# Retention and a PReLU feed-forward layer on one core: a weight piece loaded by columns, a pass-on begun on two banks, two of seven products exchanged

## The chip, the core and the metric

The kernel runs on one core of a Trainium2 chip. A core has a matrix engine (TensorE, PE in the profile, its weight loads PEld), a vector engine (VectorE, DVE), a scalar engine (ScalarE, ACT), a general engine (GpSimd, POOL), and SyncE (SP), which here only issues transfers. The metric is the device time of one execution in microseconds (us), as the median of several runs; lower is better.

## The reference

```python
# q, k, v: (4, 8, 768, 64);  w_in: (512, 2048);  w_out: (2048, 512);  alpha: (2048,)
gamma = 1.0 - 2.0 ** (-5.0 - np.arange(H))
for t in range(S):
    state = gamma * state + einsum('bhd,bhe->bhde', k[:, :, t], v[:, :, t])
    y[:, :, t] = scale * einsum('bhd,bhde->bhe', q[:, :, t], state)
x = y.transpose(0, 2, 1, 3).reshape(3072, 512)
h = x @ w_in
g = np.maximum(h, 0.0) + alpha * np.minimum(h, 0.0)
out = g @ w_out
```

A linear attention with a decaying state gives a row of 512 values for each of 3072 tokens; two matrix products with a PReLU between them follow.

## The kernel before

**Blocks and stages.** The 3072 tokens are six blocks of 512 (`NBLK`, L40). Attention is done in chunks of 128 tokens, written in pairs; the first four pairs (`w`, functions that begin with `u`) are handled as units of 256 tokens. Its result y lands in two banks of the accumulator memory PSUM, and is passed on to `xT[n]`, the block's input of the first layer, as f16. The first layer of block n (`ffn1`, `ffn1_half`, `ffn1_mix`) multiplies `w_in_all` by `xT[n]` in tiles of 128 hidden units, and the PReLU is a ScalarE instruction (`hm`) with a VectorE one (`gt`). The second layer multiplies `gt` by `w_out_all`.

**PSUM.** There are eight banks. Four rotate under the tags p0 to p3: `ps(tag="pb")` (L96) takes the next one and counts in `turns`, and `bank(i, name)` (L93) names one by its number, modulo four. The other four rotate under the tag pa for attention.

**Loads.** All inputs go through a ring of twelve staging buffers (`ring`, L102) by transfers that SP issues in program order. `load_first` (L1076) brings the first 512 columns of w_in as two transfers of 256 columns, each with all four groups of 128 rows. `load_w("wi", 1)` (L1052) brings the next 512 columns, the second piece, as two transfers of two row groups with all 512 columns. `cast_first` and `cast_w` (L1082, L1065) turn the staged f32 into f16, one instruction a row group, on the engines in the list given. The second piece's casts are three on POOL (L1172) and one on ScalarE, which stands before the last part of block 0's first tiles (L1183). `ffn1(0, lo=4)` (L1197) then goes through tiles 4 to 15: tiles 4 to 7 use the second piece, 8 to 11 the third.

**The pass-on.** `out_second` (L317) and `uout_copy` (L573) write y's two banks, ya (X = 0) and yb (X = 1), to `xT`. Where part of the state's contribution was computed ahead in a third and fourth bank and copied out (`z_copy`, L601), each bank is passed on in two halves: VectorE adds z to one (`put_y`, L611; L584) and ScalarE copies the other (L612; L585), first for X = 0, then for X = 1. Where there is no z, ScalarE copies both whole (L608; L591). The tile framework orders two engines that read the same bank.

**Seven products.** For blocks 1 to 5 the second layer is done by `seven(n)` (L802): a 2 by 2 scheme over halves of tokens, hidden units and output columns that needs seven products in place of eight, with sums of `gt` (`g_sums`, L782: which = 0 is sm[0], 1 is sm[1] made from it, 2 is `third`, 3 changes part of `gt` in place) and sums of w_out (`wsum`). A `product` is 16 matmuls of 128 by 128 by 256. Before:

```python
b, a = bank(k, "ops"), bank(k + 1, "ops")
yield from product(b, A(0, 0), W(0, 0), True)     # P1
s1 = kept(b, "um0")
yield from product(a, A(0, 1), W(1, 0), True)     # P2
store = put(0, 0, a, s1)
yield from product(b, sm[1], wsum[1])             # P3
u2 = kept(b, "um0")
```

`kept` (L825, instruction L827) is ScalarE's copy of a bank to SBUF; `put` (L833) is VectorE's sum into an output buffer (L839), and returns the store (L843), on SP or, in the last block, partly on ScalarE. P4 (sm[0]·wsum[0]) goes into c, bank k+1; P5 (third·wsum[2]) adds to b; P6 goes into d, bank k+2; P7 adds to c.

**Order.** Everything is ordered by hand. `seven(n)` is a generator that yields after each matmul, and `tick(gen, m)` (L1027) advances it by m matmuls; between the ticks stands the attention work for the next block. What follows a product (a copy, a sum, a store) is issued when the generator is next advanced. In block 1 the ticks are 17, 16, 31, then the outputs of the first pair (`out_first`, `out_second`) with states and scores of the second pair, then 6, 23, the second pair's outputs, 7 and the rest. In blocks 2 to 4 they are 34, 26, the first pair's outputs, 6, 15, 17, the second pair's outputs, 7 and the rest (L1346 to L1415). In block 5 there is no attention, and the products follow each other after 34 ticks and four VectorE sums. Each engine runs its instructions in program order.

Of the kernel before, what the change touches and what calls it, by code (L numbers as in the profile page):

```python
# [11 lines left out]
COPY = mybir.ActivationFunctionType.Copy  # L12
RELU = mybir.ActivationFunctionType.Relu
MULT = mybir.AluOpType.mult
ADD = mybir.AluOpType.add
# [4 lines left out]
def kernel(  # L20
# [10 lines left out]
    nc = tc.nc  # L31
# [10 lines left out]
    scale = 1.0 / np.sqrt(D)  # L42
# [50 lines left out]
    def bank(i, name, dt=FP, n=512):  # L93
        return psp.tile([128, n], dt, tag=f"p{i % 4}", bufs=1, name=name)
# [222 lines left out]
    def out_second(us):  # L317
        if us[0] not in zs:
            out_states(us, 1)
        z = zs.pop(us[0], None)  # L320
        yv, _ = ys.pop(us[0])
        nb, at = divmod(us[0], UB)
        if at == 0:
            xT[nb] = sbp.tile([128, 2, NP, TB // 2], F16, tag="xT", bufs=2, name=f"xT{nb}")
        to = xT[nb][:, at // 2].rearrange("p a (t x j) -> p a t x j", x=2, j=64)
        for X in range(2):
            put_y(to[:, :, :, X, :], yv[X], X, z and z[X])

    ustaged, ukq, ukT, uv, um = {}, {}, {}, {}, {}

# [242 lines left out]
    def uout_copy(w, shared=False, z=None):  # L573
        y = uy.pop(w)[0]
        nb, at = divmod(2 * w, UB)
        if at == 0:
            xT[nb] = sbp.tile([128, 2, NP, TB // 2], F16, tag="xT", bufs=2, name=f"xT{nb}")
        for X in range(2):
            lo = C * X
            to = xT[nb][:, at // 2, :, lo : lo + C].rearrange("p a (n j) -> p a j n", j=2)  # L580
            src = y[X].rearrange("p (a j n) -> p a j n", j=2, n=64)
            if z and z[X]:
                own, other = slice(2 * X, 2 * X + 2), slice(2 - 2 * X, 4 - 2 * X)
                nc.vector.tensor_tensor(out=to[:, other], in0=src[:, other], in1=z[X], op=ADD)  # L584
                nc.scalar.activation(  # L585
                    out=to[:, own], in_=src[:, own], func=COPY, bias=0.0, scale=1.0
                )
            elif shared and X == 0:
                nc.vector.tensor_copy(out=to, in_=src)
            else:  # L590
                nc.scalar.activation(out=to, in_=src, func=COPY, bias=0.0, scale=1.0)  # L591
# [11 lines left out]
        nc.scalar.activation(out=t, in_=b[:, 0:256], func=COPY, bias=0.0, scale=1.0)  # L603
        return t

    def put_y(to, src, X, z):
        if z is None:
            nc.scalar.activation(out=to, in_=src, func=COPY, bias=0.0, scale=1.0)  # L608
            return
        own, other = slice(2 * X, 2 * X + 2), slice(2 - 2 * X, 4 - 2 * X)  # L610
        nc.vector.tensor_tensor(out=to[:, other], in0=src[:, other], in1=z, op=ADD)  # L611
        nc.scalar.activation(out=to[:, own], in_=src[:, own], func=COPY, bias=0.0, scale=1.0)  # L612

    gts = {}

# [186 lines left out]
    def seven(n):  # L802
        gt, sm = gts[n], gsum[n]

        def product(bank, a, w, first=False):
            for t in range(2):
                for f in range(HF):
                    bk = bank[t] if isinstance(bank, list) else bank
                    nc.tensor.matmul(  # L809
                        out=bk[:, 256 * t : 256 * t + 256],  # L810
                        lhsT=a[:, f, 128 * t : 128 * t + 128],
                        rhs=w[:, f, :],
                        start=first and f == 0 and (t == 0 or bk is not bank),
                        stop=(f == HF - 1),
                        skip_group_check=True,
                    )
                    yield

        def A(i, j):
            return gt[:, HF * j : HF * j + HF, 256 * i : 256 * i + 256]  # L820

        def W(j, l):
            return w_out_all[:, HF * j : HF * j + HF, 256 * l : 256 * l + 256]

        def kept(bank, tag):  # L825
            t = sbp.tile([128, 512], FP, tag=tag, bufs=2, name="kept")
            nc.scalar.activation(out=t, in_=bank, func=COPY, bias=0.0, scale=1.0)  # L827
            return t

        end = n + 1 == NBLK  # L830


        def put(i, l, x, y, op=ADD, ts=(0, 1), store=None):  # L833
            os_sb = sbp.tile([128, d_model], FP, tag="os", bufs=5, name="os")
            parts = [slice(256 * t, 256 * t + 256) for t in ts]
            if not isinstance(x, list):
                parts, x = [slice(0, 512)], [x]
            for at in parts:
                nc.vector.tensor_tensor(  # L839
                    out=os_sb[:, at], in0=x[at.start // 256][:, at], in1=y[:, at], op=op  # L840
                )
            rows = slice(TB * n + 256 * i + 128 * ts[0], TB * n + 256 * i + 128 * ts[-1] + 128)
            return lambda: (store or (nc.scalar if end else nc.sync)).dma_start(  # L843
                out=out[rows, 256 * l : 256 * l + 256].rearrange("(t p) c -> p t c", p=128),
                in_=os_sb[:, 256 * ts[0] : 256 * ts[-1] + 256].rearrange(
                    "p (t c) -> p t c", c=256
                ),
            )

        k = turns[0]  # L850
        b, a = bank(k, "ops"), bank(k + 1, "ops")
        yield from product(b, A(0, 0), W(0, 0), True)
        s1 = kept(b, "um0")
        yield from product(a, A(0, 1), W(1, 0), True)
        store = put(0, 0, a, s1)
        yield from product(b, sm[1], wsum[1])
        u2 = kept(b, "um0")
        store()
        c = bank(k + 1, "ops")
        if end:  # L860
            c = [c, ps("ops")]
        yield from product(c, sm[0], wsum[0], True)
        yield from product(b, third[0], wsum[2])
        u3 = kept(b, "um1")
        store = put(1, 1, c, u3)
        d = bank(k + 2, "ops")
        turns[0] = k + 2
        yield from product(d, A(1, 1), wsum[3], True)
        store()
        store = put(1, 0, u3, d, SUB)  # L870
        if end:
            gen = product(c, A(0, 1), W(1, 1))
            for _ in range(HF):
                yield next(gen)
            store()
            put(0, 1, c, u2, ts=(0,), store=nc.sync)()
            yield from gen
            put(0, 1, c, u2, ts=(1,))()
        else:
            yield from product(c, A(0, 1), W(1, 1))  # L880
            store()
            late_stores.append(put(0, 1, c, u2))
# [144 lines left out]
    def tick(gen, m):  # L1027
        for _ in range(m):
            if next(gen, 1) == 1:
                return  # L1030
# [19 lines left out]
    wst = {}  # L1050

    def load_w(nm, i, parts=2):  # L1052
        n = 4 // parts
        for j in (0, 2):
            t = ring(f"{nm}{i}{j}").rearrange("p (j d) -> p j d", j=2)
            if nm == "wi":
                src = wi[:, j : j + 2, 512 * i : 512 * i + 512]
            else:
                src = wo[:, 4 * i + j : 4 * i + j + 2, :]
            for jj in range(0, 2, n):  # L1060
                nc.sync.dma_start(out=t[:, jj : jj + n], in_=src[:, jj : jj + n])
            for jj in range(2):
                wst[nm, i, j + jj] = t[:, jj]
# [9 lines left out]
                eng.tensor_copy(out=to, in_=t)  # L1073


    def load_first():  # L1076
        for c in range(2):
            t = ring(f"wi0{c}").rearrange("p (j d) -> p j d", j=4)
            nc.sync.dma_start(out=t, in_=wi[:, :, 256 * c : 256 * c + 256])
            wst["first", c] = t  # L1080

    def cast_first(c, engs):  # L1082
        t = wst.pop(("first", c))
        for j, eng in zip(range(4), engs):
            to = w_in_all[:, j, 256 * c : 256 * c + 256]
            if eng is nc.scalar:
                eng.activation(out=to, in_=t[:, j], func=COPY, bias=0.0, scale=1.0)
            else:
                eng.tensor_copy(out=to, in_=t[:, j])
# [24 lines left out]
    uload(1, "kq", parts=2)  # L1114
    uload(0, "v", parts=2)
    uload(1, "v", parts=2)
    load_first()
    load_w("wi", 1)
    load_w("wi", 2)
    busy(3)  # L1120
    busy(15, cols=128)
# [45 lines left out]
    uout_copy(0)  # L1167
    ustates(1, tag="pb")
    usum1(1)
    cast_first(0, [A, G, G, G])  # L1170
    cast_first(1, [A, G, A, G])
    cast_w("wi", 1, [G, G, G])  # L1172
    uload(2)
    uout_inner(1)
    uout_states(1, 0)
# [4 lines left out]
    for half in range(2):  # L1180
        for f in (0, 2):
            if half and f:
                cast_w("wi", 1, [A])  # L1183
            for _ in ffn1_half(0, half, f, f + 2):
                pass
    cast_w("wi", 2, [G, G, G, G])
# [7 lines left out]
    uscaled(2, "q", 1, G)  # L1194
    uload(3)
    load_w("wo", 3)
    for _ in ffn1(0, lo=4):  # L1197
        pass
    w_sums(0, V)
    gen = ffn2_start(0)  # L1200
# [73 lines left out]
    for n in range(1, NBLK):  # L1274
# [36 lines left out]
            pq = scores(us)  # L1311
            states(us)
        for p, w in (
            ((0, 1), (1, 0), (1, 1)) if n == 1 else ((None, 0), (None, 1)) if more else ((1, 0), (1, 1))
        ):
            g_sums(n, p, w, V)
        gen = seven(n)
# [129 lines left out]
```

## Time and profile before

| what | value |
|---|---|
| median of 3 runs | 198.67 us (197.17 to 201.42) |
| the profiled execution, its own time | 198.98 us |
| its span in the profile | 197.0 us |
| PE busy | 189.3 us (96%) |
| PEld, DVE, ACT, POOL busy | 131.7, 151.3, 121.7, 147.5 us |
| read from and written to memory | 27.35 MB, 6.29 MB |

In a timeline row the columns are the start and the length in us, the engine, the line, the operation, out<-in, the shapes and xcount, the number of merged instructions; in brackets stands how long the engine had been idle before, and what released it. A wait row gives the waiting engine and line, whom it waited for, the us in total, how many times and the longest. A row of a window gives from:to, its length, the busy share of PE, PEld, DVE, ACT and POOL with the number of instructions, the granted clock of TensorE (1.00 is full speed), the mean share of the 16 transfer engines that was busy, and GB/s. Durations in rows by group are in ns.

### The profile page before, as it was taken

What the parts mean: (1) busy time and instruction counts of PE and PEld (TensorE: products, weight loads), DVE (VectorE), ACT (ScalarE), POOL (GpSimd) and SP (SyncE); (2) the same over time, 40 slices, a digit from 0 to 9 for tenths busy, and PEclk for the clock granted to TensorE, in tenths of its full rate; (3) what the DMA queues carried; (4) which work ended last, traced back from release to release, by engine and by line L of the source; (5) the groups of instructions that cost most, each with busy time, mean ns of one, the idle gap of its engine ahead of it and who ended that gap; (6) DMA issues with size and microseconds to landing.
All of it is one profiled execution on the core that took longest, in us unless ns stands there. A gap on an engine that the chain in (4) does not pass through costs nothing.

```text
span 197.0 us, 6461 instructions
## 1 busy us (share of the span) xinstructions
PE 189.3 (96%) x2668; PEld 131.7 (67%) x2668; DVE 151.3 (77%) x260; ACT 121.7 (62%) x272; POOL 147.5 (75%) x148
## 2 busy tenths in 40 slices
PE   7789899999999989999999999999999999999993
PEld 5657444557768878744688754788754888654882
DVE  2597889253999698588897879968879977799943
ACT  3368664349687863476458988749987433687120
POOL 3286788999996955999659999579999397589000
PEclk9999999999999999999999999999999999999999
DMA  6999999999999989899999999993890011200014
GB/s 168 310 336 350 404 396 296 332 358 179 210 230 148 214 257 272 196 215 299 196 231 228 226 185 265 237 221 93 113 263 2 3 57 63 100 3 0 2 57 160
DMA packets 92749, 38.78 MB, mean 197 GB/s; under 512 B 70176, under 2 KB 88624, under 8 KB 92720
## 3 DMA queue, kind: packets, MB, share of 16 engines
q1 hardware_dynamic: 91440, 37.36, 77.2%
q10 hardware_dynamic: 1280, 1.01, 1.5%
q8 instruction: 21, 0.34, 0.7%
q14 instruction: 8, 0.07, 0.1%
HBM read 27.35 MB, written 6.29 MB: 171 GB/s over the span
## 4 chain that ended last, share of the span: by engine, by line
PE 73%; SPq 10%; DMA 7%; POOL 6%; DVE 1%; issue 1%; POOLq 0%
PE ops L809 30%; PE hps L942 16%; PE hps L632 12%; PE hps L972 5%; SPq L340 4%; SPq L117 4%; DMA wi<-in_moe_w_in_dram 4%; PE ops L734 4%; POOL wsum L757 3%; DMA kqs<-in_q_dram 3%; PE ya L293 1%; PE yb L293 1%; POOL gs L757 1%; DVE gs L757 1%; POOL ukq L354 1%; PE sca L234 1%
## 5 line engine op out<-in xcount | busy, mean ns | idle before, releaser
L809 PEld LDWEIGHTS <-gt 128*128 128x128 f16 x320 | 30.6, 98 | 4.2
L942 PE MATMUL hps<-xT,win 128*128 128x512 f16 x144 | 33.0, 379 | 0.0
L929 DVE SCALAR_TENSOR_TENSOR gt<-hm,small,hps 128x512 f16<-128x512 f32 (+1 forms) x42 | 28.7, 706 | 5.1 <-ACT hm L925 3.8
L809 PE MATMUL ops<-wout,gt 128*128 128x256 f16 x240 | 28.4, 273 | 0.0
L925 ACT ACTIVATE hm<-hps 128x512 f32<-128x512 f32 x39 | 23.1, 593 | 6.1 <-PE hps L942 5.4
L632 PE MATMUL hps<-xT,win 128*128 128x512 f16 x112 | 24.7, 379 | 0.6 <-POOL win L1073 0.6
L137 POOL TENSOR_TENSOR kq<-kqs,tab 128x512 f16<-128x512 f32 x23 | 23.7, 1051 | 1.9 <-DMA kqs<-in_q_dram 1.9
L642 DVE SCALAR_TENSOR_TENSOR gt<-hm,small,hps 128x512 f16<-128x512 f32 x28 | 20.9, 748 | 3.8 <-ACT hm L641 0.9
L942 PEld LDWEIGHTS <-win 128*128 128x128 f16 x144 | 14.1, 98 | 14.5
L641 ACT ACTIVATE hm<-hps 128x512 f32<-128x512 f32 x28 | 16.7, 597 | 8.9 <-PE hps L632 8.6
L674 DVE SCALAR_TENSOR_TENSOR gt<-hm,small,hps 128x256 f16<-128x256 f32 x40 | 16.9, 476 | 5.0 <-ACT hm L669 5.0
L827 ACT ACTIVATE kept<-ops 128x512 f32<-128x512 f32 x15 | 9.0, 597 | 18.8 <-PE ops L809 18.7
L632 PEld LDWEIGHTS <-win 128*128 128x128 f16 x112 | 10.9, 98 | 13.6 <-POOL win L1073 1.1
L809 PE MATMUL ops<-wsum,gs 128*128 128x256 f16 x160 | 19.0, 273 | 0.7 <-DVE gs L757 0.7
L217 POOL TENSOR_TENSOR t<-ss,tab 128x256 f16<-128x256 f32 x13 | 8.7, 669 | 13.6 <-DVE ss L215 13.6
L757 POOL TENSOR_TENSOR gt<-gt,gs 128x1024 f16<-128x1024 f16 x8 | 17.0, 2126 | 2.2 <-DVE gs L757 2.2
L660 PE MATMUL hps<-xT,win 128*128 128x256 f16 x160 | 18.4, 273 | 0.0
L129 ACT ACTIVATE kq<-kqs,tab 128x64 f16<-128x64 f32 x72 | 18.0, 336 | 0.0
L660 PEld LDWEIGHTS <-win 128*128 128x128 f16 x160 | 15.4, 98 | 2.6 <-DVE xT L584 0.3
L809 PEld LDWEIGHTS <-gs 128*128 128x128 f16 x160 | 15.1, 98 | 3.0 <-DVE gs L757 1.0
L669 ACT ACTIVATE hm<-hps 128x512 f32<-128x512 f32 x20 | 11.8, 597 | 4.5 <-PE hps L660 4.4
L839 DVE TENSOR_TENSOR os<-ops,kept 128x512 f32<-128x512 f32 (+1 forms) x17 | 10.5, 624 | 5.0 <-ACT kept L827 3.7
(139 smaller groups left out, 391.5 us busy)
## 6 DMA issues: line engine op xcount, KB each, us to landing
out_dram<-os SPq DMA_DIRECT2D x20, 256.0 KB, 3.6
wi<-in_moe_w_in_dram SPq DMA_DIRECT2D x8, 512.0 KB, 8.6
wo<-in_moe_w_out_dram SPq DMA_DIRECT2D x8, 512.0 KB, 8.7
kqs<-in_k_dram SPq DMA_DIRECT2D x16, 256.0 KB, 4.4
kqs<-in_q_dram SPq DMA_DIRECT2D x16, 256.0 KB, 4.3
vs<-in_v_dram SPq DMA_DIRECT2D x16, 256.0 KB, 4.7
ku<-in_k_dram SPq DMA_DIRECT2D x4, 256.0 KB, 4.4
qu<-in_q_dram SPq DMA_DIRECT2D x4, 256.0 KB, 5.3
```

Of the source, the lines that this page charges most:

```text
L129: eng.activation(out=kqs[u][:, a, h % 4, h // 4, :], in_=staged[u][nm][:, h, :], func=COPY, bias=0.0, scale=tab[:, H * a + h : H * a + h + 1],
L137: eng.tensor_tensor(out=kqs[u][:, a].rearrange("p i r d -> p r i d"), in0=staged[u][nm].rearrange("p (r i) d -> p r i d", i=4), in1=tab[:, ...
L632: nc.tensor.matmul(out=hps, lhsT=w_in_all[:, hp, 128 * ft : 128 * ft + 128], rhs=xT[n][:, :, hp, :], start=(hp == 0), stop=(hp == 3),)
L641: nc.scalar.activation(out=hm, in_=hps, func=RELU, bias=0.0, scale=-1.0)
L642: nc.vector.scalar_tensor_tensor(out=gt_at(n, ft, slice(0, TB)), in0=hm, scalar=oma_sb[:, ft : ft + 1], in1=hps, op0=MULT, op1=ADD,)
L660: nc.tensor.matmul(out=hps[:, 256 * (ft - f0) : 256 * (ft - f0) + 256], lhsT=w_in_all[:, hp, 128 * ft : 128 * ft + 128], rhs=xT[n][:, half ...
L674: nc.vector.scalar_tensor_tensor(out=gt_at(n, f, to), in0=hm[:, at], scalar=oma_sb[:, f : f + 1], in1=hps[:, at], op0=MULT, op1=ADD,)
L757: eng.tensor_tensor(out=out, in0=a, in1=b, op=op)
L809: nc.tensor.matmul(out=bk[:, 256 * t : 256 * t + 256], lhsT=a[:, f, 128 * t : 128 * t + 128], rhs=w[:, f, :], start=first and f == 0 and ( ...
L925: nc.scalar.activation(out=t, in_=src, func=RELU, bias=0.0, scale=-1.0)
L929: nc.vector.scalar_tensor_tensor(out=gt_at(n, f, cols), in0=hm, scalar=oma_sb[:, f : f + 1], in1=src, op0=MULT, op1=ADD,)
L942: nc.tensor.matmul(out=hps, lhsT=w_in_all[:, hp, 128 * ft : 128 * ft + 128], rhs=x[:, :, hp, :], start=(hp == 0), stop=(hp == 3),)
```

## The change

Three edits are made together.

1. The second piece of w_in is loaded like the first: two transfers of 256 columns with all four row groups. Its casts become three on POOL and one on ScalarE for each 256 columns. The first ScalarE cast stands where the single one stood; the second comes after tile 4 of `ffn1(0, lo=4)`.
2. The pass-on of y with z is crossed: VectorE adds to ya's part first while ScalarE copies yb's part first, and then they change banks. Where only yb has a z, ScalarE copies yb's part, then ya whole, and VectorE's add follows in program order.
3. In `seven`, P4 comes before P3. P2 goes into bank k+2 and P4 into bank k+1, and the first store comes after P4. In block 1 the order of VectorE's sums is changed to suit: its half of sm[0] first, then the two halves of sm[1].

```diff
-        for X in range(2):
-            put_y(to[:, :, :, X, :], yv[X], X, z and z[X])
+        put = [(to[:, :, :, X, :], yv[X]) for X in range(2)]
+        if z:
+            put_crossed(put, z)
+            return
+        for x, y in put:
+            nc.scalar.activation(out=x, in_=y, func=COPY, bias=0.0, scale=1.0)
...
+    def put_crossed(put, z):
+        own, other = [slice(0, 2), slice(2, 4)], [slice(2, 4), slice(0, 2)]
+
+        def add(X):
+            to, src = [a[:, other[X]] for a in put[X]]
+            nc.vector.tensor_tensor(out=to, in0=src, in1=z[X], op=ADD)
+
+        def copy(X, at):
+            to, src = [a[:, at] for a in put[X]]
             nc.scalar.activation(out=to, in_=src, func=COPY, bias=0.0, scale=1.0)
...
+        if z[0] is not None:
+            add(0)
+        copy(1, own[1])
+        copy(0, slice(0, 4) if z[0] is None else own[0])
+        add(1)
...
         k = turns[0]
-        b, a = bank(k, "ops"), bank(k + 1, "ops")
+        b, a = bank(k, "ops"), bank(k + 2, "ops")
         yield from product(b, A(0, 0), W(0, 0), True)
         s1 = kept(b, "um0")
         yield from product(a, A(0, 1), W(1, 0), True)
         store = put(0, 0, a, s1)
-        yield from product(b, sm[1], wsum[1])
-        u2 = kept(b, "um0")
-        store()
         c = bank(k + 1, "ops")
         if end:
             c = [c, ps("ops")]
         yield from product(c, sm[0], wsum[0], True)
+        store()
+        yield from product(b, sm[1], wsum[1])
+        u2 = kept(b, "um0")
         yield from product(b, third[0], wsum[2])
         u3 = kept(b, "um1")
         store = put(1, 1, c, u3)
...
-    def load_first():
-        for c in range(2):
+    def load_columns(i):
+        for c in range(2 * i, 2 * i + 2):
             t = ring(f"wi0{c}").rearrange("p (j d) -> p j d", j=4)
             nc.sync.dma_start(out=t, in_=wi[:, :, 256 * c : 256 * c + 256])
-            wst["first", c] = t
+            wst["columns", c] = t
...
-    load_first()
-    load_w("wi", 1)
+    load_columns(0)
+    load_columns(1)
...
-    cast_first(0, [A, G, G, G])
-    cast_first(1, [A, G, A, G])
-    cast_w("wi", 1, [G, G, G])
+    cast_columns(0, [A, G, G, G])
+    cast_columns(1, [A, G, A, G])
+    cast_columns(2, [G, G, G])
+    cast_columns(3, [G, G, G])
...
-                cast_w("wi", 1, [A])
+                cast_columns(2, [A], [3])
...
-    for _ in ffn1(0, lo=4):
+    gen = ffn1(0, lo=4)
+    tick(gen, 4)
+    cast_columns(3, [A], [3])
+    for _ in gen:
         pass
...
-            ((0, 1), (1, 0), (1, 1)) if n == 1 else ((None, 0), (None, 1)) if more else ((1, 0), (1, 1))
+            ((1, 0), (0, 1), (1, 1)) if n == 1 else ((None, 0), (None, 1)) if more else ((1, 0), (1, 1))
```

`cast_columns` is `cast_first` with a choice of row groups. `uout_copy` is edited as `out_second` is.

More of the change, by code (lines that the diff above doesn't have):

```diff
@@ L577, in uout_copy @@
             xT[nb] = sbp.tile([128, 2, NP, TB // 2], F16, tag="xT", bufs=2, name=f"xT{nb}")
+        put = []
         for X in range(2):
@@ L580, in uout_copy @@
             to = xT[nb][:, at // 2, :, lo : lo + C].rearrange("p a (n j) -> p a j n", j=2)
[L581 to L588, printed above, removed]
+            put.append((to, y[X].rearrange("p (a j n) -> p a j n", j=2, n=64)))
+        if z:
+            put_crossed(put, z)
+            return
+        for X, (to, src) in enumerate(put):
+            if shared and X == 0:
                 nc.vector.tensor_copy(out=to, in_=src)
@@ L604, in z_copy @@
         return t
[L606 to L612, printed above, removed]
+    def put_crossed(put, z):
[5 more added lines that the diff above has]
+            to, src = [a[:, at] for a in put[X]]
+            nc.scalar.activation(out=to, in_=src, func=COPY, bias=0.0, scale=1.0)
+        if z[0] is not None:
[3 more added lines that the diff above has]
+        add(1)
     gts = {}
@@ L1073, in cast_w, with cast_columns @@
                 eng.tensor_copy(out=to, in_=t)
-    def load_first():
-        for c in range(2):
+    def load_columns(i):
+        for c in range(2 * i, 2 * i + 2):
             t = ring(f"wi0{c}").rearrange("p (j d) -> p j d", j=4)
             nc.sync.dma_start(out=t, in_=wi[:, :, 256 * c : 256 * c + 256])
-            wst["first", c] = t
-    def cast_first(c, engs):
-        t = wst.pop(("first", c))
-        for j, eng in zip(range(4), engs):
+            wst["columns", c] = t
+    def cast_columns(c, engs, js=range(4)):
+        t = wst["columns", c]
+        for j, eng in zip(js, engs):
             to = w_in_all[:, j, 256 * c : 256 * c + 256]
```

## The prediction

> **What bounds the kernel now.** I read first the page's chain that ended last, by engine, then the whole list of waits of the weight loads (PEld, whose idle time shows a held TensorE most plainly), then the timeline around each place that the change touches.
>
> ```profile
> PE 73%; SPq 10%; DMA 7%; POOL 6%; DVE 1%; issue 1%; POOLq 0%
> PEld L632 <- POOL win L1073: 1.1, 1, 1.1
> PEld L972 <- ACT kept L985: 1.1, 3, 0.4
> PEld L809 <- DVE gs L757: 1.0, 1, 1.0
> PEld L660 <- DVE xT L584: 0.3, 1, 0.3
> ```
>
> TensorE carries 73% of the chain that ends last. Once it has begun on the big products it is held by other engines only a handful of times: once by POOL's cast of w_in, once by VectorE's sums for a seven-product block, briefly by y's pass-on, and three times by ScalarE's copies in the mixed first layer. So a stall that the change adds to TensorE lengthens the kernel by its whole length, and a stall that it takes away shortens it, unless the next supplier is as late.
>
> **The exchange: what it takes away.** Call the products P1 to P7 in the order of before. P3 (sm[1]·wsum[1], into bank b) needs the second sum; P4 (sm[0]·wsum[0], into c) needs only the first, from which the second is made. The one wait on sums is in block 1:
>
> ```profile
> 66.61 2.12 POOL L757 TENSOR_TENSOR gs<-gt 128x1024 f16<-128x1024 f16 x1
> 69.38 0.68 DVE L757 TENSOR_TENSOR gs<-gt 128x1024 f16<-128x1024 f16 x1
> 69.56 0.60 PE L809 MATMUL ops<-wsum,gs 128*128 128x256 f16 x4
> 70.09 0.69 DVE L757 TENSOR_TENSOR gs<-gs,gt 128x1024 f16<-128x1024 f16 x1
> 70.84 3.23 PE L809 MATMUL ops<-wsum,gs 128*128 128x256 f16 x28 [0.68 <-DVE gs L757]
> ```
>
> P3's first four matmuls run at 69.56, the fifth waits for the sum that ends at 70.78. P4 in its place needs POOL's half of sm[0], there at 68.73, and VectorE's half, which the new order makes first. Matmuls of this size follow each other by 0.109 us (32 in 3.66 us, below: (3.66 - 0.273) / 31), so the fifth would start at 70.00: **gain 0.84 us** (0.68 by the idle column, 0.96 by the loads). P3 comes 16 x 0.109 = 1.75 us after P4's start at 69.56, at 71.3, when its sum is ready. P2 moves to bank k+2, so P4's bank has no reader left. The first store keeps its place in the count of matmuls; in blocks 1 to 4 it stays on SP, in the last it now stands on ScalarE ahead of the copy u2 instead of behind it, its sum being made long before. I cost both at nothing.
>
> **The exchange: what it adds.** P3 and P5 (third·wsum[2]) both go into bank b, and between them ScalarE must copy b out (u2, L827), since P5 adds on top. P4 lay between and covered that copy with 1.75 us of matmuls. Now P5 follows P3 at once and waits for the copy. In the last block nothing else is queued on ScalarE:
>
> ```profile
> 185.04 3.66 PE L809 MATMUL ops<-wsum,gs 128*128 128x256 f16 x32
> 187.05 0.60 ACT L827 ACTIVATE kept<-ops 128x512 f32<-128x512 f32 x1 [2.96 <-PE ops L809]
> 188.54 1.91 PE L809 MATMUL ops<-wsum,third 128*128 128x256 f16 x16
> ```
>
> P3's 16th matmul started at 185.04 + 15 x 0.109 = 186.68 and ends 0.273 later, at 186.95; the copy starts 0.10 after that and takes 0.60. As second of the two, P3 ends at 188.70, the copy at 189.40. How soon TensorE goes on after such a copy, the mixed first layer shows:
>
> ```profile
> 113.63 0.60 ACT L985 ACTIVATE kept<-hps 128x512 f32<-128x512 f32 x1 [0.20 <-PE hps L972]
> 114.28 0.33 PEld L972 LDWEIGHTS <-wins 128*128 128x128 f16 x4 [0.32 <-ACT kept L985]
> ```
>
> 0.05 us after its end. P5 then starts at 189.46 in place of 188.54: **loss 0.92**.
>
> In blocks 1 to 4 the boundary between P3 and P5 lies at the 64th matmul of the generator. It comes inside, or at the start of, the six ticks that follow the attention work of the first pair, and the generator issues the copy only when it is asked for the 65th matmul. So u2's copy stands on ScalarE behind the two pass-on copies of y (L608), which themselves wait for products only just done:
>
> ```profile
> 75.50 0.60 ACT L608 ACTIVATE xT<-ya 128x512 f16<-128x512 f32 x1 [0.41 <-PE yb L293]
> 75.68 1.92 PE L809 MATMUL ops<-wsum,third 128*128 128x256 f16 x16
> 75.99 0.59 ACT L608 ACTIVATE xT<-yb 128x512 f16<-128x512 f32 x1
> ```
>
> ```profile
> 104.32 0.60 ACT L608 ACTIVATE xT<-ya 128x512 f16<-128x512 f32 x1 [0.54 <-PE yb L293]
> 104.56 2.00 PE L809 MATMUL ops<-wsum,third 128*128 128x256 f16 x16
> 104.81 0.59 ACT L608 ACTIVATE xT<-yb 128x512 f16<-128x512 f32 x1
> 105.29 1.15 ACT L150 ACTIVATE vx<-vs 128x512 f16<-128x512 f32 x2
> ```
>
> ```profile
> 133.07 0.60 ACT L608 ACTIVATE xT<-ya 128x512 f16<-128x512 f32 x1 [0.58 <-PE yb L293]
> 133.30 1.91 PE L809 MATMUL ops<-wsum,third 128*128 128x256 f16 x16
> ```
>
> ```profile
> 161.74 0.60 ACT L608 ACTIVATE xT<-ya 128x512 f16<-128x512 f32 x1 [0.53 <-PE yb L293]
> 162.02 1.91 PE L809 MATMUL ops<-wsum,third 128*128 128x256 f16 x16
> ```
>
> The next instruction on ScalarE starts 0.97 us after the first L608 (105.29 - 104.32). Put u2's copy there: it ends 0.60 later, and P5 starts 0.05 after that, 1.62 us after the first L608. Block 1: 77.12 for 75.68, loss 1.44. Block 2: 105.94 for 104.56, 1.38. Block 3: 134.69 for 133.30, 1.39. Block 4: 163.36 for 162.02, 1.34. (The places shift as a whole with what went before; L608 waits for TensorE itself, so the differences stay.) Sum with the last block: **loss 6.47 us**. Behind the waiting P5 stand P6, P7, the second pair's products and the next block's first layer; everything waits, since all of it is TensorE's. Bounds: at least a bare round trip of 0.92 in each of five places, 4.6; at most 1.5 in four and 1.0 in the last, 7.0. I take 6.5, made from rows of the same places.
>
> **w_in's second piece.** Two transfers of 512 KB stay two of 512 KB at the same place in SP's queue, each now four row groups by 256 columns. The casts of 512 columns (three on POOL, one on ScalarE) become six on POOL and two on ScalarE of 256.
>
> ```profile
> 15.20 2.13 POOL L1089 CAST win<-wi 128x256 f16<-128x256 f32 x5
> 18.95 1.17 POOL L1073 CAST win<-wi 128x512 f16<-128x512 f32 x2 [1.62 <-DMA wi<-in_moe_w_in_dram]
> 20.55 0.59 PE L632 MATMUL hps<-xT,win 128*128 128x512 f16 x2
> 21.08 0.61 POOL L1073 CAST win<-wi 128x512 f16<-128x512 f32 x1 [0.96 <-DMA wi<-in_moe_w_in_dram]
> 21.66 0.61 POOL L457 TENSOR_TENSOR ut<-uss,tab 128x256 f16<-128x256 f32 x1
> 21.75 5.57 PE L632 MATMUL hps<-xT,win 128*128 128x512 f16 x25 [0.60 <-POOL win L1073]
> 22.21 3.08 POOL L1073 CAST win<-wi 128x512 f16<-128x512 f32 x5
> ```
>
> TensorE does two matmuls of tile 4 and stops until the second transfer is in and cast. They follow by 0.216 us ((5.57 - 0.379) / 24), so the third could start at 20.98: up to 0.77 to gain, as the first 256 columns now come whole at 18.95. But POOL must cast three quarters of the second column pair after 21.08, some 0.4 us each by the first row (2.13 / 5 = 0.43 with the overlaps), and L457 and the third piece stand behind it. L457 moves from 21.66 to about 22.3, the third piece's first cast from 22.21 to 22.8, its fourth ends at 22.8 + 4 x 0.61 = 25.2. Tile 8's last matmul needs that one; in before it ran at 21.75 + 17 x 0.216 = 25.4. So what tile 4 gains, tile 8 gives back: **net about 0**. Bounds: a gain of 0.77 if the columns land 0.8 earlier, and below that a loss. For the loss:
>
> ```profile
> 16.00:17.00 1.00, 0.82 (x24) 0.48 (x23) 0.79 (x3) 1.00 (x4) 1.00 (x4) 1.00 0.91 273
> 19.00:20.00 1.00, 1.00 (x11) 0.90 (x10) 1.00 (x3) 0.72 (x2) 1.00 (x2) 1.00 1.07 404
> 21.00:22.00 1.00, 0.40 (x3) 0.13 (x3) 0.38 (x1) 0.95 (x2) 0.92 (x2) 1.00 1.05 408
> ```
>
> The stretch after 16 us, in which the first piece's short rows give way to the second's, moved 273 GB/s (last column) and the long rows at 19 us 404. 1.05 MB at 273 takes 3.8 us, at 404 2.6: a second piece in short rows would be late by at most 1.2 us, and tile 8 with it. I take 0, between the ends, because the slow stretch is as well one of long rows. The Trainium skill, DMA: Bandwidth & Descriptors, section Specifications, puts line rate at 512 bytes a row and above; by it the 1 KB rows cost nothing and the term is 0 as taken, while the 273 speaks for the loss.
>
> **The pass-on on different banks.** The wait list's L660 row (0.3 us) is y of unit 2; the rest lies beside other work, as here:
>
> ```profile
> 109.39 0.42 DVE L611 TENSOR_TENSOR xT<-ya,zs 128x256 f16<-128x256 f32 x1 [0.36 <-ACT zs L603]
> 109.85 0.38 ACT L612 ACTIVATE xT<-ya 128x256 f16<-128x256 f32 x1 [0.23 <-DVE xT L611]
> 110.18 0.38 ACT L612 ACTIVATE xT<-yb 128x256 f16<-128x256 f32 x1
> ```
>
> ScalarE waits for VectorE to leave ya, though they write different parts. Crossed, its copy of yb starts at about 109.6 and that of ya after 109.96: it ends at 110.3 in place of 110.56, while VectorE's second add moves some 0.25 later behind the copy of yb. One side gains what the other gives. At most 0.3 at unit 2 and nothing elsewhere, in either direction; I take a gain of 0.05. The Trainium skill, PSUM — Partial Sum Buffer, section PSUM bank collisions raise a hardware error, says that any two engines on one bank are to be kept apart, readers too; the 0.23 agrees.
>
> **Sum.** 198.98 (this execution's time, 0.31 above the median of 198.67) + 6.47 - 0.84 + 0 - 0.05 = 204.6; on the median, **204.3 us**, slower by 2.8%. A measurement of this kernel can tell about 2%, 4.0 us here.
>
> **Rivals.** (1) ScalarE is not late: u2's copy finds it free in all five blocks, the stalls are bare round trips, 198.67 + 4.6 - 0.84 = 202.4, within 2%. For it: ScalarE stands idle 0.4 to 0.6 before L608, so a copy that came first would find it free. Against: program order puts L608 first. 0.13. (2) Not slower: TensorE's stalls of blocks 1 to 4 are taken up in the next first layer, if ScalarE and VectorE are what paces that and TensorE only runs ahead; it decides from a slack of 1.4 us a block. Then only the last block pays: 198.67 + 0.92 - 0.84 - 0.05 = 198.7, or 197.9 with w_in's 0.77. For it: the three L972 waits on ScalarE. Against: these are 0.4 us each and the chain is TensorE's throughout. 0.09. (3) The columns land late: 204.3 + 1.2 = 205.5. 0.10. (4) The exchange doesn't stall since something else stands between P3 and P5: only in block 1 could it, and there the generator's order speaks against it; 204.3 - 1.4 = 202.9. 0.05. (5) The stalls cost clock as well: each is followed by a stretch at half the clock, some 1.7 us lost each, 212. The windows at 21 us show a clock of 1.00 with TensorE busy 0.40; 0.02. The Trainium skill, TensorE: Matmul & The Clock Gate, section A second HAM failure mode: psum-queue depth-cycling, tells of such a loss from short idles between groups; the 1.00 disagrees.
>
> **How the numbers follow.** The forecast has 0.61. Lowest bounds: 198.67 + 4.6 - 0.96 - 0.77 - 0.3 = 201.2; highest 198.67 + 7.0 - 0.68 + 1.2 + 0.3 = 206.5. That range leaves out rivals 2 and 5. Slower by over 2% (above 202.6) takes the forecast, 3, 5, most of 4 and a little of 1: 0.79. Within 2%: the rest of 1 and 4, nearly all of 2: 0.18. Faster by over 2%: 0.03.
>
> **What would show it.** In the profile of the changed kernel TensorE's third matmuls wait on ScalarE's L827 copy five times, some 1.4 us four times and 0.9 once; the wait on VectorE's gs is gone; the wait at tile 4 is gone and a shorter one on POOL's casts stands at tile 8. A list of waits without the five would prove the forecast wrong, and so would a first layer that is shorter by what the block before it lost.

## The result, and the profile after

The changed kernel took 204.58 us (median of 6 runs, 203.42 to 207.26), the kernel before 199.06 us (6 runs, 197.17 to 202.36). The ratio is 1.031, with a 95% interval from 1.021 to 1.041: slower. It leaves out the slowest executions (two of six before, one of six after), and so isn't the quotient of the two medians, 1.028. On a second chip the same pair gave 1.035 (1.029 to 1.041). The forecast was 204.3 us, between 201.2 and 206.5.

The page's head and its chain by engine, of the changed kernel:

```profile
span 201.8 us, 6459 instructions
PE 77%; SPq 5%; ACT 4%; DMA 4%; POOL 3%; DVE 3%; issue 1%; ACTq 0%; DVEq 0%
```

ScalarE, which was not in the chain of before, now has 4% of it. The list of waits says where. In the changed kernel the products' matmuls are line 821, the copy `kept` is line 839, the pass-on without z line 331, the crossed pass-on lines 614 (add) and 618 (copy), and the seconds of the first layer are lines 672 and 984. The columns are waiter, releaser, us in total, times, longest.

```profile
PEld L821 <- issue: 6.4, 5, 1.4
PE ops L821 <- ACT kept L839: 5.8, 5, 1.4
PEld L984 <- ACT kept L997: 1.1, 3, 0.4
PEld L672 <- DVE xT L614: 0.4, 1, 0.4
```

Five waits of TensorE on the copy, 1.4 us at most, that before did not have. (The weight loads of these matmuls stand still five times too, 6.4 us in all, put down to "issue". I read them as the same stalls: in blocks 1, 2 and 5 the loads go on in the same moment as P5's first matmul (74.93, 105.18, 192.42). A matmul's own idle is counted from the modelled end of the one before, and so is shorter.) The wait on VectorE's sums (gs) is gone from the list. The timeline at the five places, of which the first, the second and the last are shown, in that order:

```profile
73.30 0.60 ACT L331 ACTIVATE xT<-ya 128x512 f16<-128x512 f32 x1 [0.41 <-PE yb L293]
73.80 0.59 ACT L331 ACTIVATE xT<-yb 128x512 f16<-128x512 f32 x1
74.28 0.60 ACT L839 ACTIVATE kept<-ops 128x512 f32<-128x512 f32 x1
74.93 0.81 PE L821 MATMUL ops<-wsum,third 128*128 128x256 f16 x6 [1.38 <-ACT kept L839]
...
103.55 0.60 ACT L331 ACTIVATE xT<-ya 128x512 f16<-128x512 f32 x1 [0.54 <-PE yb L293]
104.05 0.59 ACT L331 ACTIVATE xT<-yb 128x512 f16<-128x512 f32 x1
104.53 0.60 ACT L839 ACTIVATE kept<-ops 128x512 f32<-128x512 f32 x1
105.18 1.03 PE L821 MATMUL ops<-wsum,third 128*128 128x256 f16 x8 [1.23 <-ACT kept L839]
...
191.77 0.60 ACT L839 ACTIVATE kept<-ops 128x512 f32<-128x512 f32 x1 [4.70 <-PE ops L821]
192.42 0.81 PE L821 MATMUL ops<-wsum,third 128*128 128x256 f16 x6 [0.75 <-ACT kept L839]
```

In blocks 1 and 2 one sees the queue on ScalarE: two pass-on copies, then u2's, then P5. In block 5 the copy stands alone. P5 starts 1.63 us after the first pass-on copy in both of the first two places (74.93 - 73.30, 105.18 - 103.55).

Where the 4.8 us between the two profiled spans went, read from the timelines as the time from the first matmul of P1 to the first matmul of the next first layer (in block 5, to the end of VectorE's last sum):

| stage | before | after | difference |
|---|---|---|---|
| start to P1 of block 1 | 66.06 | 64.88 | -1.18 |
| seven products, block 1 | 15.67 | 16.08 | +0.41 |
| seven products, block 2 | 14.40 | 15.70 | +1.30 |
| seven products, block 3 | 14.35 | 15.73 | +1.38 |
| seven products, block 4 | 14.37 | 15.70 | +1.33 |
| seven products, block 5 | 12.87 | 13.77 | +0.90 |
| the four first layers between them | 56.68 | 56.41 | -0.27 |
| last sum to the end | 2.60 | 3.53 | +0.93 |

Block 1 holds both the new wait and the one removed. The row ahead of block 1 is where the second piece is loaded, of which more below. The last two rows are not the exchange's doing, as the last section shows: the first layers give 0.27 us back and the end of the kernel, when the matmuls and sums are done and only stores are left, is 0.93 us longer. VectorE's last sum, before and after:

```profile
193.98 0.42 DVE L839 TENSOR_TENSOR os<-ops,kept 128x256 f32<-128x256 f32 x1 [0.45 <-PE ops L809]
197.85 0.42 DVE L851 TENSOR_TENSOR os<-ops,kept 128x256 f32<-128x256 f32 x1 [0.45 <-PE ops L821]
```

It ends at 194.40 of a span of 197.0, and at 198.27 of 201.8.

### The profile page after: what moved, and what is told of

It reads as the page before. It is cut to its first block, busy times and chain, and to the rows that moved or that the text cites. A ratio compares the mean times of both kernels' runs of the same rounds, so it can differ in the third digit from the quotient of the medians.

```text
span 201.8 us, 6459 instructions
## 1 busy us (share of the span) xinstructions
PE 188.3 (93%) x2668; PEld 131.6 (65%) x2668; DVE 152.4 (76%) x260; ACT 121.3 (60%) x273; POOL 148.1 (73%) x151
## 4 chain that ended last, share of the span: by engine, by line
PE 77%; SPq 5%; ACT 4%; DMA 4%; POOL 3%; DVE 3%; issue 1%; ACTq 0%; DVEq 0%
PE ops L821 27%; PE hps L954 15%; PE hps L644 8%; PE hps L672 8%; PE ops L746 5%; PE hps L984 5%; SPq L117 2%; DMA qu<-in_q_dram 2%; SPq L344 2%; DMA vs<-in_v_dram 2%; PE ops L708 2%; POOL wins L769 2%; ACT xT L331 2%; ACT kept L839 1%; PE ya L293 1%
```

## The experiments

Theory: TensorE stands still before P5 until ScalarE has copied bank b, in four blocks behind two other copies. Rivals: the loss is shared with the other two edits; the new order of products costs in itself; P5 is held by something else.

**The exchange alone (e1).** Edit: before, with `seven` and block 1's order of sums as in the change, nothing else.

> Before with the exchange alone (P4 ahead of P3, P2 in bank k+2, and block 1's order of sums), w_in and the pass-on as before. My theory, that the added time is TensorE waiting for u2's copy before P5: slower than before by 6.5 - 0.8 = 5.6 us, and the profile lists five waits of P5 on that copy, about 1.4 us four times and 0.9 once. Rival, that the loss is shared with the other two edits (late columns, crossed adds): slower by under 4 us.

Measured: 1.035 of before (1.028 to 1.042), that is 6.9 us on 197.92. The same five waits:

```profile
PEld L809 <- issue: 6.4, 5, 1.4
PE ops L809 <- ACT kept L827: 5.8, 5, 1.4
```

The exchange by itself makes a loss as large as that of all three edits, and more than the 5.6 us expected (5.5 to 8.3 by the interval); the rival of under 4 us falls.

**The other two edits alone (e2).** Edit: the changed kernel with the order of before in `seven` and in block 1's sums.

> The changed kernel with the exchange undone (products and sums in the order of before), columns and crossed pass-on kept. My theory as predicted: w_in's term about 0, so within 0.5 us of before. Second reading, from the changed kernel's trace, where the first block-1 product starts 1.1 us earlier than in before: faster by about 0.8 us. Rival, that the two edits cost: slower by 1 us or more.

Measured: 1.003 (1.000 to 1.007, the lower end just below 1). That is 0.6 us slower, between -0.1 and 1.4: not the 0.8 us of gain that the profiled start promised, while the rival's cost of 1 us is not excluded. The 0.27 us won and 0.93 us lost in the last two rows of the table come to much the same, 0.66. Its profile shows the mechanism that the forecast gave for tile 8. These are POOL's casts and TensorE's matmuls on the second and third piece:

```profile
20.86 1.10 POOL L1101 CAST win<-wi 128x256 f16<-128x256 f32 x3 [1.76 <-DMA wi<-in_moe_w_in_dram]
22.47 4.09 POOL L1085 CAST win<-wi 128x512 f16<-128x512 f32 x7
24.81 6.43 PE L644 MATMUL hps<-xT,win 128*128 128x512 f16 x29 [0.17 <-POOL win L1085]
```

The third piece's casts begin at 22.47, the fourth of them ends near 24.9, and TensorE stops at its twentieth matmul, the last of tile 8 (the other 29 follow).

**The copy covered (e3).** Edit, on the changed kernel:

```diff
-        yield from product(b, sm[1], wsum[1])
-        u2 = kept(b, "um0")
+        u2s = []
+        yield from product(b, sm[1], wsum[1], done=lambda: u2s.append(kept(b, "um0")))
+        u2 = u2s[0]
...
-                tick(gen, 26)
+                tick(gen, 30)
...
-            tick(gen, 6)
+            tick(gen, 6 if n == 1 else 2)
```

`product` calls `done` after its 16th matmul, before it yields.

> The changed kernel with one difference: in blocks 2 to 4 P3 is finished ahead of the first pair's outputs (ticks 34, 30, 2 in place of 34, 26, 6), and in all blocks u2's copy is issued with P3's last matmul, so that it stands ahead of the two pass-on copies on ScalarE and the outputs of the first pair cover it. My theory: the four waits of blocks 1 to 4 vanish, 5.5 us, and only the last block's 0.9 stays; faster than the changed kernel by 5.5 and within 1 us of before. Rival, that the order P4, P3 costs in itself (banks, sums) or the queue on ScalarE isn't what sets the 1.4: under 3 us come back.

Measured: 1.008 (1.003 to 1.013). Against the 1.031 and 1.035 of the changed kernel, 4.7 to 5.4 us came back. Of the five waits one is left:

```profile
PEld L821 <- issue: 0.9, 1, 0.9
PE ops L821 <- ACT kept L841: 0.7, 1, 0.7
```

It is the last block's. P4 still stands ahead of P3, and the products of blocks 2 to 4 take 14.41, 14.44 and 14.37 us, as in the kernel before. So the order as such costs nothing that shows here; what costs is that nothing stands between P3 and P5.

**Another order of sums (e4).** Edit: e2, with block 1's sums in the order (1, 0), (1, 1), (0, 1).

> Columns and crossed pass-on kept, products in the order of before, and block 1's sums on VectorE in the order sm[0] second half, sm[1] second half, sm[1] first half, so that only the last of them stands behind POOL's sum. My theory: P3's wait in block 1 (0.84 us) goes without any exchange, and no wait on u2 arises: faster than the same kernel with the old order of sums by 0.8, faster than before by 0.8 to 1.6. Rival, that POOL's half ends too late for either order: same as with the old order of sums, and the wait of P3 on VectorE's gs stays near 1 us.

Measured: 1.005 (1.001 to 1.010), where e2 has 1.003: faster than neither before nor e2. In the stretch of block 1 the wait on the sums is 0.2 us, where the first profile of before had 1.0:

```profile
PEld L821 <- DVE gs L769: 0.2, 1, 0.2
```

But e2's profile, with the old order of sums, has no wait on these sums at all, so this doesn't show that the new order took anything away. What the wait depends on shows the next kernel.

**Before once more (f3).** No edit.

> The kernel before again, for a second profile of the same program: whether the second transfer of w_in's second piece lands at about 21 us as in the first profile, and how long TensorE then stops at tile 4. If landings are the execution's luck, both move by 0.5 us or more; if they follow from the rows' length, 18.9 and 21.0 come again within 0.3 relative to the first piece.

Measured: 197.43 us, span 195.4. POOL, then TensorE, at the second piece and at block 1's products:

```profile
18.00 1.17 POOL L1073 CAST win<-wi 128x512 f16<-128x512 f32 x2 [0.55 <-DMA wi<-in_moe_w_in_dram]
20.02 0.61 POOL L1073 CAST win<-wi 128x512 f16<-128x512 f32 x1 [0.85 <-DMA wi<-in_moe_w_in_dram]
20.33 10.52 PE L632 MATMUL hps<-xT,win 128*128 128x512 f16 x48
...
64.67 2.13 POOL L757 TENSOR_TENSOR gs<-gt 128x1024 f16<-128x1024 f16 x1 [0.48 <-DVE gt L674]
65.32 3.67 PE L809 MATMUL ops<-wout,gt 128*128 128x256 f16 x32
68.83 3.66 PE L809 MATMUL ops<-wsum,gs 128*128 128x256 f16 x32
```

The second transfer is cast at 20.02 and not at 21.08, and all 48 matmuls run without a stop (their weight loads were held for 0.3 us). POOL's sum begins at 64.67, where in the first profile it began at 66.61, and P3 follows P2 without a wait. So this execution has neither of the two waits that the change takes away.

They are not rare either. The stop at tile 4 stands also in e1, which loads the second piece as before: cast at 21.52, a stop of 1.1 us. The wait on the sums stands also in f4, 0.8 us, and is missing in e2. It goes with the start of POOL's sum. Where that lies behind P1's first matmul, by 0.55 us in the first profile (66.61, 66.06) and 0.43 in f4, TensorE waits; where it lies 0.65 ahead, here and in e2, TensorE doesn't. In f4 TensorE came early, P1 at 64.97, and waited for the sums instead. So a gain read from one profile is not one of the median. This bears on why the edits show no gain in the runs and why the changed kernel's loss by ratio, 6.2 and 6.9 us, is nearer the bare 6.4 than the sum's 5.6; the end's 0.93 us, which is in these losses too, is another part of it.

**Columns alone (f4).** Edit: before, with the new loads and casts of the second piece.

> Before with the second piece by columns alone. Forecast as predicted: about 0, within 0.5 us of before, with the wait at tile 4 gone and a shorter one at tile 8 in executions where the columns land late. Second reading, from the changed kernel's trace: 0.8 faster. Rival, late columns: slower by up to 1.2.

Measured: 1.002 (0.999 to 1.005): about nothing, as forecast. TensorE stops at neither tile 4 nor tile 8 in its profile.

**The queue on ScalarE taken away (f1, g1).** Edit, on the changed kernel:

```diff
                 states(pb)
+                tick(gen, 6)
                 out_second(pa)
             else:
                 states(pb)
+                tick(gen, 2)
                 out_second(pa)
...
-            tick(gen, 6)
+            tick(gen, 4 if n == 1 else 0)
```

The first branch is that of blocks 2 to 4, the second that of block 1.

> The changed kernel with the ticks that end P3 and begin P5 put ahead of the first pair's out_second (six in blocks 2 to 4, two of the six in block 1), so that u2's copy stands ahead of the two pass-on copies on ScalarE while P5 still follows P3 at once. Theory, that 0.9 of each wait is the bare round trip and the other 0.5 is the queue on ScalarE: the four waits fall from about 1.4 to 0.9, in block 1 to 0.4 or less since other products then partly stand between, so 1.5 to 2.5 us faster than the changed kernel and still 3 to 4 slower than before. Rival, that the whole 1.4 is the way through PSUM and semaphores: the waits stay at 1.4.

Measured: 1.030 (1.025 to 1.034), that is 5.9 us slower than before, not the 3 to 4 expected, and hardly faster than the changed kernel's 1.031 and 1.035. The profiled execution ran at a granted clock of 0.854 and lasted 223.0 us, so its times say little. The same kernel beside the changed one is g1:

> The kernel with u2's copy ahead of the pass-on copies again, since its first profile ran at a granted clock of 0.85: five waits of 4.2 us in all there, 0.9 at most. Theory: 4.0 to 4.3 us of waits at full clock too, and on the same chip 1.5 to 2.3 faster than the changed kernel. Rival, that what the waits lose comes back elsewhere, since P5's first matmuls now hold up the first pair's out_second: the waits fall and the time stays within 0.7 us of the changed kernel.

> The changed kernel again beside the two others, for a second profile and a comparison on one chip. Theory: the five waits on u2's copy come again at 6.4 us in all, within 0.2, whatever the landings of that execution; slower than before by 5.5 to 7.

Measured on one chip: g1 1.025 (1.020 to 1.029), g2, the changed kernel, 1.035 (1.029 to 1.041); 2.0 us between them, with intervals that just touch. The waits of g1's matmuls on the copy were 3.5 us in five, 0.7 at most, and g2's were as in the first profile, 5.8 in the matmuls and 6.4 in the loads. Block 2 of g1:

```profile
102.95 0.60 ACT L839 ACTIVATE kept<-ops 128x512 f32<-128x512 f32 x1 [0.87 <-PE ops L821]
103.60 0.38 PE L821 MATMUL ops<-wsum,third 128*128 128x256 f16 x2 [0.69 <-ACT kept L839]
103.91 0.20 PEld L293 LDWEIGHTS <-t 64*64 64x64 f16 x12 [0.21 <-issue]
104.15 1.43 PEld L821 LDWEIGHTS <-third 128*128 128x128 f16 x14
```

The copy stands first, and what is left is the round trip: about 0.5 of each 1.4 was time behind the queue. Of this little came back as time. Block 1's products became 0.8 us shorter (16.16 to 15.35), those of blocks 2 to 4 only 0.08, 0.04 and 0.22 (from 15.70, 15.74, 15.71). That is 1.15 us of the 2.3 by which the two profiled spans differ (202.8 and 200.5); the rest lies ahead of block 1, where g1 came to P1 at 64.69 and g2 at 65.81. So outside block 1 the rival is right: what the waits lose comes back elsewhere. Part of it can be seen. Cutting the big products in two puts two more changes between 128-wide and 64-wide matmuls in each block, and the third row above shows one of them, 0.21 of idle. The Trainium skill, TensorEngine Tiling (Array Packing), section Key Properties, says that a change of tiling mode drains TensorE; the 0.21 agrees, though no run here shows that this is its cause.

**The copy doubled (g3).** Edit: the changed kernel, with u2's copy done a second time over itself.

> The changed kernel with u2's copy done twice, the second time over itself, so that P5 waits for one more copy of the bank. Theory, that P5 stands still until ScalarE has let go of bank b: each of the five waits grows by 0.49 to 0.6, 2.5 to 3 us slower than the changed kernel. Rival, that P5 is held by something else in that place (a later sum, instruction supply): no change, within 0.7 us.

Measured on the same chip: 1.047 (1.040 to 1.053) against 1.035, 2.4 us more, with intervals that just touch; 2.5 to 3 was expected. Each wait grew by about 0.64, where 0.49 to 0.6 was expected:

```profile
PEld L821 <- issue: 9.6, 5, 2.0
PE ops L821 <- ACT kept L875: 8.9, 5, 2.0
```

TensorE waits for ScalarE's last hold on bank b, copy by copy. If something else held P5, a second copy would have changed nothing.

**Both (f2).** Edit: e3, and in the last block P3 before P4 as in before.

> Columns, crossed pass-on, the covered exchange in blocks 1 to 4 (P3 finished and u2's copy issued ahead of the first pair's outputs), and P3 before P4 in the last block as in before. Theory: no wait on u2 is left at all and block 1's wait on the sums is gone, so 0.9 us faster than the covered exchange in all blocks and 0.3 to 1.5 faster than before. Rival, that what is left of the loss in the covered kernel isn't the last block's copy: same time as the covered kernel, about 0.8% above before.

Measured: 1.000 (0.998 to 1.003), and no wait on u2 in its list. The step from e3's 1.008 (1.003 to 1.013) is 0.7%, 1.4 us, where 0.9 was expected; the two were run on different chips and their intervals overlap a little. It brings all the loss back, but not the 0.3 to 1.5 us of gain that was expected: none of the versions beats the kernel before.

## Why the prediction was right, step by step

**The new wait** was the right term and the right size: five waits, predicted 1.44, 1.38, 1.39, 1.34 and 0.92, 6.47 in all, measured 6.4 at the loads. The offset of 1.62 us from the first pass-on copy came out at 1.63. Against the second profile of before, which has no wait on sums, block 1's products are 1.43 us longer (14.65 to 16.08), for a forecast of 1.44. The bare round trip has its runs (e3 and g3). For the queue g1 shows that the waits shrink with it, but not that the time does, outside block 1.

**The wait taken away** was sized at 0.84 from its rows, and in that execution it was there. As a term for the median it was too large: of the four profiles with the old order of products and sums (before, f3, f4, e2) two have the wait and two don't. The step that erred took a wait seen in one execution for a property of the program.

**The number** is closer than its terms. Of the sum's gains the runs show nothing clear of noise, 0.84 and 0.05 us, and the longer end, 0.93 us, was not in the sum; the median before also came out 0.39 us higher, at 199.06, than the 198.67 that the sum started from. That 204.58 was measured for 204.3 is in part luck. By ratio the change costs 3.1% and 3.5%, for 2.8% forecast.

**The second piece** at about nothing is what f4 and e2 measure, 0.2% and 0.3%. In the profiled execution of the changed kernel TensorE reached block 1 earlier by 1.18 us, which looked like a gain of the edit:

```profile
18.02 1.10 POOL L1101 CAST win<-wi 128x256 f16<-128x256 f32 x3 [0.64 <-DMA wi<-in_moe_w_in_dram]
19.38 1.09 POOL L1101 CAST win<-wi 128x256 f16<-128x256 f32 x3 [0.26 <-DMA wi<-in_moe_w_in_dram]
20.26 10.52 PE L644 MATMUL hps<-xT,win 128*128 128x512 f16 x48
20.98 4.70 POOL L1085 CAST win<-wi 128x512 f16<-128x512 f32 x8
```

The columns were there at 19.38, earlier than forecast, so neither tile 4 nor tile 8 waited. But the kernel before can come earlier too, at 65.32 in f3 for 66.06, and f4, with P1 at 64.97, is not faster in the runs. The giving back at tile 8 showed itself only where the columns landed late (e2, 0.17 us; g2, cast at 20.58, 0.2 us at the loads). The fear of late short rows (rival 3), 1.2 us, found no support: the second transfer's cast began between 19.16 and 21.23 us in the ten profiles by columns, and between 20.02 and 21.52 in the three with long rows.

**The pass-on** went as described:

```profile
109.99 0.42 DVE L614 TENSOR_TENSOR xT<-ya,zs 128x256 f16<-128x256 f32 x1 [0.43 <-PE yb L293]
110.06 0.37 ACT L618 ACTIVATE xT<-yb 128x256 f16<-128x256 f32 x1
110.44 0.38 ACT L618 ACTIVATE xT<-ya 128x256 f16<-128x256 f32 x1
110.46 0.42 DVE L614 TENSOR_TENSOR xT<-yb,zs 128x256 f16<-128x256 f32 x1
```

The two engines work side by side and change banks; all four instructions are done 0.89 us after the first start (110.88 - 109.99), where before took 1.17 (110.56 - 109.39). Unit 2's wait of 0.3 is 0.4 now, so the 0.05 us of gain was not won there. By itself the edit wasn't run; with the columns it makes no difference that can be measured. What it may do elsewhere, against the forecast's "nothing", stands in the last section.

**The rivals.** ScalarE not being late (1) is refuted by the 1.4, and something else standing between P3 and P5 in block 1 (4) by the 1.38 there. The first layers taking up the loss (2) is refuted by e1, where they are as long as before (56.79 and 56.68 us). Clock lost to stalls (5) is refuted by a granted clock of 1.0 in the changed kernel's profile; the 1.7 us a stall that this rival reckoned with appear in no run, and with five of them its sum is 212.8 rather than 212.

## What to carry to other kernels

When two groups of matmuls add into the same bank and a copy must be taken between them, what stands between them in TensorE's order is the cover of that copy; moving it away costs a round trip, and the copy waits besides for whatever is queued ahead of it on its engine. With generators, look at when the copy is issued: here it came only with the next matmul asked for, behind two other copies. Profile the kernel before more than once: a wait that stands in one execution and not in the next is not yet a gain.

## What the runs showed that was not expected

The cast that waits for the second transfer of w_in's second piece began at 21.08, 20.02 and 21.52 us in three executions with long rows (before, f3, e1) and anywhere from 19.16 to 21.23 in ten by columns, so single landings can't price an edit of this size.

The longer end was not looked for. From VectorE's last sum to the end of the span it is 2.57 to 2.59 us in the four profiles without the crossed pass-on (before, f3, f4, e1) and 3.50 to 3.52 in eight with it; f1, at its lower clock, has 3.20. In the changed kernel the store that SP issues last lands 2.75 us after its issue, in before 1.87. In the same way the four first layers come to 56.4 or 56.5 us with the crossed pass-on and 56.7 or 56.8 without it, f1 aside. Columns alone (f4) and the exchange alone (e1) have neither, so the crossed pass-on, or its company with the columns, brings both. Why it should lengthen the end stays open, and no run has it alone.

One execution of f1 had a granted clock of 0.85 from 10 us on, 0.854 in the mean, on a program of one core, where the same program also ran at 0.995 to 1.0; its cause stays open.
